# Moving one transposition, one reciprocal and one subtraction in an attention and MLP kernel on Trainium2

## The chip, the cores and the metric

The kernel runs on one core of one Trainium2 chip. The metric is the device time of one execution in microseconds (us), the median of three runs. The engines are TensorE (PE, with its weight loads shown apart as PEld), VectorE (DVE), ScalarE (ACT), GpSimd (POOL) and SyncE (SP), which issues all DMAs of this kernel.

## What is computed

Three stages follow each other: an attention with a relative-position bias, and two MLP mixers. Only the attention bears on this change.

```python
scores = scale * np.matmul(q, k.transpose(0, 1, 3, 2))      # B=4, H=8, S=576, D=64
x = (psi_rel / psi_i)[..., None]
h = np.maximum(x @ w1 + b1, 0.0)                            # hidden = 32
bias = h @ w2                                               # one value per head and pair of positions
scores = scores + bias.transpose(2, 0, 1)[None, :, :, :]
scores = scores - np.max(scores, axis=-1, keepdims=True)
attn = np.exp(scores)
attn = attn / (np.sum(attn, axis=-1, keepdims=True) + 1e-09)
out = np.matmul(attn, v)
```

The MLP weights arrive as 64-bit floats. The kernel rebuilds 32-bit floats from the two words and then splits each weight into a high part (rounded to fp32r) and a low part (the difference), for products in three terms.

## The kernel before

**Units and passes.** The attention is cut into 80 units. A unit is one pair of heads of one batch and one block of 128 rows (the last block of a sequence, index NM, has 64 rows, and both heads then share one tile). The first batch has the units 0 to 19, in the order of `order0`: the 64-row block first, all four pairs of heads, then the next block. The main loop (line 608) runs n from -3 to 80. A pass n does, in this order of the program: the reciprocal and normalisation of unit n+2 (`normalise`, line 459), the scores and minima of unit n+3 (`scores`, line 422), the transpositions of unit n (`turn`, line 482), the transposition of q for unit n+5 (`q_turn`, line 389; first batch only, later batches transpose q on VectorE), the exponentials of unit n+3 (`softmax`, line 450), and the products with v of unit n-1 (`values`, line 507) with their placement in X (`place`, line 415).

**Signs.** The scores are kept negated, so the maximum is a minimum: L443 adds the bias to the scores in PSUM and takes the row minimum, once for each head of a unit. L454 is the exponential with its sum, L460 adds the small constant to the sum on GpSimd, L461 is the reciprocal on VectorE, and L467 scales the rows on GpSimd.

**The bias.** It is built once, in 36 groups of 16 positions. `hidden` (line 315) makes the hidden layer of a group, three of four parts on VectorE (L325) and one on ScalarE (L327); `bias_product` (line 340) multiplies it by w2 on TensorE (L344) into a PSUM tile; `bias_place` (line 352) evicts that tile on ScalarE (L357) and sends it by DMA on SP to `bias_m` or `bias_t`. Six groups are done ahead of the loop, then two in each of the passes -3 to 11 (`gs`).

**PSUM tiles.** `s_tile` (line 333) hands out two tiles `s0` and `s1` of two banks each in turn, to the scores and to the bias products alike; for a unit of two heads `scores` starts again with `s0`, so the scores take `s0` and `s1` and the two bias groups of the pass again `s0` and `s1`. The tile `z` (line 621) holds the transposition of a unit's last columns in `z[:, 0]` and the transposed q in `z[:, 1]`. `values` takes the tags `o` and `z` for its two results (line 514), so it needs z free again. The names `q` and `z` in rows of the trace are these tiles: L394 transposes q into z, L404 copies it out, L487 transposes the unit's last columns into z and L488 copies them out.

**Order on the engines.** Every engine runs its instructions in the order of the program; the kernel sets that order by hand and only waits are added. In a pass with bias groups ScalarE runs: the copy of z (L488), of x (L495), of q (L404), the first exponential (L454), the two evictions (L357), the second exponential, the copy of a values result (L419), two parts of hidden layers (L327). TensorE runs: scores (L435), z, x, y (L487, L494, L500), q (L394), products of both groups (L344), values (L519 to L526).

**Weight parts.** `Jobs` (line 62) prepares MLP weights in pieces between passes. A job of 64-bit weights is four pieces of work on VectorE (L121, L127, L131, L136) and a square on ScalarE (L120). `finish` (line 95) makes the high and low part by `split` (line 57): L59 on ScalarE rounds, L60 subtracts, in `finish` on GpSimd. It is called in the second piece of the next job, ahead of L127:

```python
                yield
                self.finish()
                V.scalar_tensor_tensor(
                    out=wi_, in0=up_, scalar=-0x40000000, in1=wi_, op0=ALU.bitwise_and, op1=ALU.bitwise_or
                )
```

During the attention seven jobs run: three parts of the first weight (`t1`), in the passes from 28 on whose n - 20 is 0 or 3 modulo 5, and four parts of the second (`t2`), one or two pieces a pass from pass 72 on. The first two of them are finished in the passes 40 and 50. The jobs of the later stages (`c1`, `c2`, `wi`, `wo`) use the same class.

Of the kernel before, what the change touches and what calls it, by code (L numbers as in the profile page):

```python
# [7 lines left out]
F32 = mybir.dt.float32  # L8
# [11 lines left out]
def kernel(ctx, tc, ins, consts, out, dbg=None, nb=4, stop=None):  # L20
# [41 lines left out]
    class Jobs:  # L62


        def __init__(self, stg, ahead):
            self.stg, self.ahead = stg, ahead
            self.queue, self.loaded, self.next, self.open, self.gen = [], {}, 0, None, None
            self.done = set()

        def add(self, key, nm, rows, cols, fold, dst, times=1):  # L70

# [23 lines left out]
        def finish(self):  # L95
            if self.open is None:
                return
            key, wf, dst = self.open
            hi, lo = dst()
            if len(hi.shape) == 3:  # L100
                wf = wf.rearrange("p (a b) -> p a b", a=hi.shape[1])
            split(wf, hi, lo, G)
            self.done.add(key)
            self.open = None

# [227 lines left out]
    def s_tile(name):  # L333
        flip[0] ^= 1
        return ps_s.tile([P, 2, 512], F32, tag=f"s{1 - flip[0]}", name=name)
# [1 line left out]
    t = pp.tile([P, 2 * N + TL], F32, tag="p", name="early")  # L337
    early = {groups[2 * j + 1]: t[:, j * N:(j + 1) * N] for j in range(2)}

    def bias_product(gi, hs):  # L340
        ps = s_tile("bps")
        for c in range(4):
            for hf in range(2):
                T.matmul(  # L344
                    ps[32 * c:32 * c + 32, hf, 0:HN],
                    lhsT=w2b.rearrange("p g h -> p (g h)"),
                    rhs=hs[c][:, hf * HN:(hf + 1) * HN],
                    start=True, stop=True, tile_position=(0, 32 * c),
                )
        return ps  # L350
# [35 lines left out]
        V.transpose(out=kt, in_=kraw.pop((b, p)))  # L386
        keys[b, p] = kt

    def q_turn(n, z):

        b, p, it = units[n]
        w = P if it < NM else TL
        if b == 0:
            T.transpose(z[:, 1, 0:w], qraw.pop((b, p, it)), ident[0:w, 0:w])  # L394
        else:
            queries[n] = turned(b, p)[:, it * P:it * P + w]

    def q_out(n, z):
        b, p, it = units[n]
        if b > 0:  # L400
            return
        w = P if it < NM else TL
        t = hl_p.tile([P, P], F32, tag="q0", name="q0", bufs=5)[:, 0:w]
        S.copy(out=rows(t, w), in_=dealt(z[:, 1, 0:w], w))  # L404
        queries[n] = t


# [11 lines left out]
        S.copy(out=out, in_=b)  # L419
        return lambda: V.tensor_tensor(out=out, in0=a, in1=out, op=ALU.add)  # L420

    def scores(n):
        b, p, it = units[n]
        qt, kt = queries.pop(n), keys[b, p]
        na = 2 if it < NM else 1
        if na == 2:
            flip[0] = 0
        ss = [s_tile("ss") for a in range(na)]

        for hf in range(2):  # L430
            js = slice(hf * HN, (hf + 1) * HN)
            for m in range(na):
                for a in range(2):
                    r, o = halves[a], halves[m if na == 2 else a]
                    T.matmul(  # L435
                        ss[a % na][o, hf, 0:HN], lhsT=qt[r, m * HD:(m + 1) * HD], rhs=kt[r, js], start=True, stop=True
                    )
        bias = [bias_m[:, it, 2 * p + a] for a in range(2)] if na == 2 else [bias_t[:, p]]
        pr = pp.tile([P, 2 * N + TL], F32, tag="p", name="pr")
        mn = sm_p.tile([P, 2], F32, tag="mn", name="mn")  # L440
        sm = sm_p.tile([P, 2], F32, tag="sm", name="sm")
        for a in range(na):
            V.tensor_tensor_reduce(  # L443
                out=pr[:, a * NB:a * NB + N].rearrange("p (f n) -> p f n", f=2), in0=ss[a][:, :, 0:HN],
                in1=bias[a].rearrange("p (f n) -> p f n", f=2),
                scale=scale, scalar=BIG, op0=ALU.add, op1=ALU.min, accum_out=mn[:, a:a + 1],
            )
        return pr, mn, sm, na

    def softmax(pr, mn, sm, na, which):  # L450
# [105 lines left out]
    for gi in range(GUP):  # L556
# [10 lines left out]
            k_parts0(p, hl_p if p < 2 else first, "" if p < 2 else "x")  # L567
        if gi >= GUP - 2:
            u = gi - (GUP - 2)
            z = ps_t.tile([P, 2, P], F32, tag="z", name="z")  # L570
            q_turn(u, z)
            q_out(u, z)
    bias_place(groups[GUP - 1], bps)
    gnext = GUP

# [32 lines left out]
    for n in range(-3, U + 1):  # L608
        gs = []
        if n >= -3 and gnext < GALL:  # L610
            gs = list(range(gnext, min(gnext + 2, GALL)))
            gnext += 2
        if 0 <= n + 2 < U:
            normalise(*st[n + 2])
        if 0 <= n + 3 < U:
            st[n + 3] = scores(n + 3)
        if len(gs) > 0:
            hide(gs[0] + 2)
        if n == U - 1:
            values(n - 1)()  # L620
        z = ps_t.tile([P, 2, P], F32, tag="z", name="z") if n < U else None
        if n == U - 1:
            early_x([NM])
        if 0 <= n < U:
# [8 lines left out]
        if n == U - 1:  # L633
            wjobs.need(("t1", NM // 2))
            ph0 = [s_tile("ph")[:, 0] for m in range(NTT)]
            tok1(x0, 0, ph0[0])
        if 0 <= n + 5 < U:
            q_turn(n + 5, z)
        bp = [bias_product(gi, hs.pop(gi)) for gi in gs]
        if 0 <= n + 5 < U:  # L640
            q_out(n + 5, z)
        if 0 <= n + 3 < U:
            softmax(*st[n + 3], which=(0,))
        if 0 <= n < U and n != U - 2:
            y_out(ys, y)
        for gi, x in zip(gs, bp):
            bias_place(groups[gi], x)

        late = 0 < n < U - 1 or n == U
        if late and not gs:  # L650
# [73 lines left out]
    while wjobs.gen is not None or wjobs.next < len(wjobs.queue):  # L724
        wjobs.step()
    wjobs.finish()
    for m in range(1, NTT):
        tok1(x0, m, ph0[m])
    for pl in (sm_p, pt_p, pp, hl_p, raw_p, apool):
# [566 lines left out]
```

## Time and profile before

| what | value |
|---|---|
| median of 3 runs | 903.33 us (903.23 to 903.37) |
| profiled execution | 903.33 us, span 901.5 us |
| PE busy | 885.4 us (98%) |
| PEld busy | 767.9 us (85%) |
| DVE busy | 614.2 us (68%) |
| ACT busy | 421.8 us (47%) |
| POOL busy | 301.3 us (33%) |
| granted TensorE clock | 1.000 |

The span runs from the first to the last instruction; the execution's time has a little around it. Busy shares are of the whole span, over stages that differ: the attention takes the first 320 us or so, the first MLP goes to about 685 us, the second to the end. A busy PE row counts a matmul from its start to its modelled end, and matmuls overlap, so it isn't PE at its peak. In a timeline each row has the start, the duration, engine, line, operation, names and shapes, and in brackets how long the engine was idle before it and what ended that.

### The profile page before, as it was taken

Reading aid. Unit: us, or ns where it says so; the run is one execution under the profiler, and the core shown is the slowest. Engines: PE = TensorE matmul, PEld = TensorE weight load, DVE = VectorE, ACT = ScalarE, POOL = GpSimd, SP = SyncE. Lnnn points to the kernel's source line nnn. Section 1 sums busy time; section 2 is a strip of 40 time slices with the busy share of each in tenths; the row PEclk is TensorE's granted clock in tenths of the full one; section 3 lists DMA queues with packets and bytes.
Section 4 is the critical chain, followed back from the end, with each engine's and each line's share of the span. In section 5 each row is a group of like instructions: output and inputs, shape, how many; then the busy total and the mean of one; then the engine's idle time right before and its main releaser. Section 6 shows DMA issues by size and latency. Waiting matters only on the chain.

```text
span 901.5 us, 22183 instructions
## 1 busy us (share of the span) xinstructions
PE 885.4 (98%) x8962; PEld 767.9 (85%) x8962; DVE 614.2 (68%) x1392; ACT 421.8 (47%) x955; POOL 301.3 (33%) x529
## 2 busy tenths in 40 slices
PE   9999999999999999999999999999999999999998
PEld 4456777767677688999999999999998989889996
DVE  7888677878777779888825353332316999896756
ACT  7999887777777754334312121211115523222310
POOL 1244566666666713133300001001002452423230
PEclk9999999999999999999999999999999999999999
DMA  8956443324323123224300100000041001010002
GB/s 187 198 122 131 92 108 55 72 57 77 64 44 68 32 68 103 85 98 130 127 1 24 47 24 24 33 15 1 1 79 47 24 1 47 1 59 1 1 13 93
DMA packets 120006, 55.39 MB, mean 61 GB/s; under 512 B 101856, under 2 KB 108640, under 8 KB 119904
## 3 DMA queue, kind: packets, MB, share of 16 engines
q1 hardware_dynamic: 119904, 53.98, 24.9%
q8 instruction: 70, 1.15, 0.5%
q14 instruction: 32, 0.26, 0.1%
HBM read 38.62 MB, written 4.72 MB: 48 GB/s over the span
## 4 chain that ended last, share of the span: by engine, by line
PE 75%; DVE 15%; ACT 6%; issue 2%; POOL 1%; DMA 0%; SPq 0%; ACTq 0%; DVEq 0%; POOLq 0%
PE a L931 14%; PE pg L768 14%; PE ss L435 8%; PE o L519 7%; PE po L1148 4%; PE pv L1042 4%; PE ps L1117 4%; PE bps L344 3%; PE x L494 3%; PE pu L1095 3%; PE y L500 3%; DVE res L886 2%; PE z L487 2%; DVE w L131 2%; ACT X L327 1%
## 5 line engine op out<-in xcount | busy, mean ns | idle before, releaser
L931 PE MATMUL a<-g,c 128*128 128x384 f32 x864 | 162.4, 335 | 1.8 <-DVE X L939 1.0
L931 PEld LDWEIGHTS a<-g,c 128*128 128x128 f32 x864 | 150.9, 188 | 3.4 <-ACT g L774 2.2
L775 DVE SCALAR_TENSOR_TENSOR g<-pg,g 128x384 fp32r<-128x384 f32 x72 | 40.0, 556 | 163.7 <-ACT g L774 163.7
L768 PE MATMUL pg<-u,c 128*128 128x384 f32 x720 | 134.4, 334 | 0.0
L467 POOL TENSOR_SCALAR pr<-pr,sm 128x576 f32<-128x576 f32 (+2 forms) x208 | 120.9, 599 | 29.9 <-DVE sm L461 27.9
L768 PEld LDWEIGHTS pg<-u,c 128*128 128x128 f32 x720 | 125.6, 188 | 0.1
L774 ACT ACTIVATE g<-pg 128x384 fp32r<-128x384 f32 x72 | 35.3, 491 | 192.2 <-PE pg L768 192.2
L454 ACT ACTIVATE pr<-pr,mn 128x576 f32<-128x576 f32 x144 | 111.8, 777 | 8.8 <-DVE mn L443 7.6
L443 DVE CUSTOM_DVE_ANT_0 pr<-ss,bias_m 128x576 f32<-128x576 f32 x128 | 90.8, 747 | 2.4 <-ACT X L327 1.8
L519 PE MATMUL o<-xA,vm 64*64 64x128 f32 (+1 forms) x1280 | 82.7, 265 | 0.0
L435 PE MATMUL ss<-kt,X 64*64 64x288 f32 x864 | 77.3, 408 | 2.2 <-DVE mn L443 2.1
L519 PEld LDWEIGHTS o<-xA,vm 64*64 64x64 f32 x1280 | 64.3, 133 | 17.6 <-issue 11.5
L520 PE MATMUL o<-yA,vm 64*64 64x128 f32 x1024 | 71.7, 276 | 0.0
L886 DVE STREAM_TRANSPOSE res<-X 32x256 f32<-32x256 f32 (+1 forms) x176 | 68.2, 387 | 2.7
L60 POOL TENSOR_TENSOR wi<-w,wi 128x512 fp32r<-128x512 f32 x8 | 14.0, 1752 | 153.0 <-DVE g L775 112.5
L60 POOL TENSOR_TENSOR c<-w,c 128x512 fp32r<-128x512 f32 x24 | 35.5, 1480 | 87.3 <-ACT c L59 77.1
L1117 PE MATMUL ps<-wsT,vn 128*128 128x288 f32 x384 | 56.6, 296 | 1.1 <-DVE tmp L1127 1.1
L520 PEld LDWEIGHTS o<-yA,vm 64*64 64x64 f32 x1024 | 55.5, 132 | 0.0
L120 ACT ACTIVATE sq<-wraw 128x512 f32<-128x512 f32 (+2 forms) x43 | 27.8, 646 | 56.7 <-DVE w L136 54.7
L1117 PEld LDWEIGHTS ps<-wsT,vn 128*128 128x128 f32 x384 | 52.7, 188 | 1.9 <-DVE tmp L1127 1.8
L495 ACT COPY xA<-x 128x512 f32<-128x512 f32 x80 | 47.0, 588 | 11.5 <-PE x L494 11.1
L1095 PEld LDWEIGHTS pu<-y,wi 128*128 128x128 f32 x384 | 51.4, 188 | 0.3
(160 smaller groups left out, 1745.0 us busy)
## 6 DMA issues: line engine op xcount, KB each, us to landing
wraw<-in_moe_w_ch_dram SPq DMA_DIRECT2D x24, 512.0 KB, 3.6
bias_m<-bst SPq DMA_DIRECT2D x32, 288.0 KB, 4.0
vm<-in_v_dram SPq DMA_DIRECT2D x32, 128.0 KB, 3.3
wraw<-in_moe_w_in_dram SPq DMA_DIRECT2D x8, 512.0 KB, 3.6
out_dram<-res SPq DMA_DIRECT2D x16, 256.0 KB, 2.0
kr<-in_k_dram SPq DMA_DIRECT2D x48, 72.0 KB, 2.4
qr<-in_q_dram SPq DMA_DIRECT2D x48, 72.0 KB, 2.5
wraw<-in_moe_w_out_dram SPq DMA_DIRECT2D x4, 512.0 KB, 3.3
```

The costliest lines, as they stand in the source:

```text
L60: (eng or V).tensor_tensor(out=lo, in0=src, in1=hi.bitcast(F32), op=ALU.subtract)
L435: T.matmul(ss[a % na][o, hf, 0:HN], lhsT=qt[r, m * HD:(m + 1) * HD], rhs=kt[r, js], start=True, stop=True)
L443: V.tensor_tensor_reduce(out=pr[:, a * NB:a * NB + N].rearrange("p (f n) -> p f n", f=2), in0=ss[a][:, :, 0:HN], in1=bias[a].rearrange("p ...
L454: S.activation(out=pr[:, a * NB:a * NB + N], in_=pr[:, a * NB:a * NB + N], func=AF.Exp, scale=-1.0, bias=mn[:, a:a + 1], accum_out=sm[:, a ...
L467: G.tensor_scalar(out=pr[:, dc:dc + hi - lo], in0=pr[:, lo:hi], scalar1=sm[:, a:a + 1], scalar2=1.0, op0=ALU.mult, op1=ALU.mult,)
L519: T.matmul(o[0:HD, 0:w], lhsT=vm[r, t, 0], rhs=xs[r, t, 0:w], start=st_, stop=en)
L520: T.matmul(o[HD:P, 0:w], lhsT=vm[r, t, 1], rhs=rh[r], start=st_, stop=en)
L768: T.matmul(pg, lhsT=c1[f][i][:, d], rhs=u[j][:, d], start=d == 0 and n == 0, stop=d == ND - 1 and n == 2)
L886: V.transpose(out=o, in_=src(c)[32 * a:32 * a + 32])
L931: T.matmul(acc[d], lhsT=c2[f][i][:, d * P:(d + 1) * P], rhs=g[j], start=f == f0 and n == 0, stop=f == f1 and n == 2,)
L1095: T.matmul(pu[:, hf, 0:HN], lhsT=wi[i][:, d, f * P:(f + 1) * P], rhs=y[j][:, d, js], start=d == 0 and m == 0, stop=d == ND - 1 and m == 2,)
L1117: T.matmul(ps[:, hf, 0:HN], lhsT=vn[i][:, t, ds_], rhs=wsT[j][:, t, js], start=t == 0 and m == 0, stop=False,)
```

## The change

Three edits.

1. The transposed q of the first batch (units n+5 below U0 = 20) no longer lies in `z[:, 1]` but in the tile of the pass's first bias group, in columns 288 to 416 of its first bank, which the products leave free. It is transposed ahead of those products, and its copy to SBUF comes behind the eviction of the first group; in the passes 12 to 14, which have no bias group, the transposition has an `s_tile` of its own and the copy comes right behind. The tile z has one half only.
2. `normalise` of unit n+2 is called between the two minima of unit n+3, not ahead of `scores`.
3. `Jobs` subtracts on VectorE until the attention is over, and on GpSimd from there on.

```diff
@@ class Jobs
             self.done = set()
+            self.eng = V
...
-            split(wf, hi, lo, G)
+            split(wf, hi, lo, self.eng)
@@ bias_product
-    def bias_product(gi, hs):
-        ps = s_tile("bps")
+    def bias_product(gi, hs, ps=None):
+        ps = s_tile("bps") if ps is None else ps
@@ q_turn, q_out
-            T.transpose(z[:, 1, 0:w], qraw.pop((b, p, it)), ident[0:w, 0:w])
+            T.transpose(zq[:, 0:w], qraw.pop((b, p, it)), ident[0:w, 0:w])
...
-        S.copy(out=rows(t, w), in_=dealt(z[:, 1, 0:w], w))
+        S.copy(out=rows(t, w), in_=dealt(zq[:, 0:w], w))
@@ scores
-    def scores(n):
+    def scores(n, between):
...
+            if a == 0:
+                between()
         return pr, mn, sm, na
@@ main loop
-        if 0 <= n + 2 < U:
-            normalise(*st[n + 2])
+        ahead = (lambda: normalise(*st[n + 2])) if 0 <= n + 2 < U else (lambda: None)
         if 0 <= n + 3 < U:
-            st[n + 3] = scores(n + 3)
+            st[n + 3] = scores(n + 3, ahead)
+        else:
+            ahead()
...
-        z = ps_t.tile([P, 2, P], F32, tag="z", name="z") if n < U else None
+        z = ps_t.tile([P, 1, P], F32, tag="z", name="z") if n < U else None
...
+        qs = s_tile("bps") if 0 <= n + 5 < U0 else None
+        zq = None if qs is None else qs[:, 0, HN:HN + P]
         if 0 <= n + 5 < U:
-            q_turn(n + 5, z)
-        bp = [bias_product(gi, hs.pop(gi)) for gi in gs]
-        if 0 <= n + 5 < U:
-            q_out(n + 5, z)
+            q_turn(n + 5, zq)
+        bp = [bias_product(gi, hs.pop(gi), qs if gi == gs[0] else None) for gi in gs]
+        if qs is not None and not gs:
+            q_out(n + 5, zq)
         if 0 <= n + 3 < U:
             softmax(*st[n + 3], which=(0,))
         if 0 <= n < U and n != U - 2:
             y_out(ys, y)
-        for gi, x in zip(gs, bp):
-            bias_place(groups[gi], x)
+        for gi, ps in zip(gs, bp):
+            bias_place(groups[gi], ps)
+            if gi == gs[0]:
+                q_out(n + 5, zq)
@@ behind the attention
     wjobs.finish()
+    wjobs.eng = G
```

The two transpositions of q ahead of the loop use a tile of one half with the same tag; nothing else changes there.

## Rows read from the trace of the kernel before

**Rows 1.** Busy time by stretches: engine, busy us, instructions, then clock, DMA share, GB/s.

```profile
50.00:75.00 25.00, 24.80 (x441) 16.22 (x440) 21.88 (x55) 23.77 (x54) 10.42 (x24) 1.00 0.48 112
```

**Rows 2.** Chain of waits in order of time, 59 to 71.5 us: start, us, what.

```profile
65.34 2.17 PE bps L344 x32
...
67.53 0.83 ACT bst L357
...
70.51 0.26 ACT zA L488
...
70.82 0.33 PE z L394
```

**Rows 3.** Timeline of TensorE: the first transposition of some passes.

```profile
40.69 0.30 PE L487 MATMUL z<-ident,pr 128*64 128x128 f32 x1
...
92.80 0.33 PE L487 MATMUL z<-ident,pr 128*128 128x128 f32 x1
98.36 0.33 PE L487 MATMUL z<-ident,pr 128*128 128x128 f32 x1
...
109.68 0.33 PE L487 MATMUL z<-ident,pr 128*128 128x128 f32 x1
...
189.54 0.33 PE L487 MATMUL z<-ident,pr 128*128 128x128 f32 x1
192.79 0.33 PE L487 MATMUL z<-ident,pr 128*128 128x128 f32 x1
197.97 0.30 PE L487 MATMUL z<-ident,pr 128*64 128x128 f32 x1
```

**Rows 4.** Timeline of TensorE's weight loads, passes 6, 11 and 12.

```profile
65.00 0.14 PEld L394 LDWEIGHTS z<-ident,qm 128*128 128x128 f32 x1 [0.31 <-ACT zA L488]
...
93.73 0.14 PEld L394 LDWEIGHTS z<-ident,qm 128*128 128x128 f32 x1
...
100.03 0.13 PEld L519 LDWEIGHTS o<-xA,vm 64*64 64x64 f32 x1 [0.23 <-ACT q L404]
```

**Rows 5.** Timeline of VectorE, minima in the passes 6 and 13.

```profile
64.52 0.08 DVE L443 DVE_READ_ACCUMULATOR2_ANT mn<- 128x1 f32 x1
...
103.07 0.76 DVE L443 CUSTOM_DVE_ANT_0 pr<-ss,bias_m 128x576 f32<-128x576 f32 x1 [0.17 <-PE x L494]
```

**Rows 6.** Timeline of ScalarE, passes 12 and 73.

```profile
99.71 0.27 ACT L404 COPY q<-z 128x128 f32<-128x128 f32 x1
...
300.96 0.40 ACT L59 CAST t<-w 128x256 fp32r<-128x256 f32 x1
```

**Rows 7.** Chain of waits in order of time, 190 to 202 us.

```profile
193.06 0.53 ACT t L59
...
193.72 1.27 POOL t L60
...
195.37 0.74 DVE pr L443
```

**Rows 8.** Timeline of VectorE, passes 40, 41 and 74.

```profile
192.54 0.68 DVE L127 SCALAR_TENSOR_TENSOR w<-wraw,w 128x512 int32<-128x512 int32 x1
195.28 0.17 DVE L461 RECIPROCAL sm<-sm 128x2 f32<-128x2 f32 x1 [2.07 <-POOL sm L460]
...
302.54 0.17 DVE L461 RECIPROCAL sm<-sm 128x2 f32<-128x2 f32 x1 [1.30 <-POOL sm L460]
```

**Rows 9.** Line 60 over the whole span: count, ns min/median/max, first and last start.

```profile
L60 DVE TENSOR_TENSOR x<-px,x x15: 674/683/684, 330.4 to 368.3; 128x512 fp32r<-128x512 f32 x12, 64x512 fp32r<-64x512 f32 x3
...
L60 DVE TENSOR_TENSOR wsT<-wst,wsT x10: 415/416/457, 690.1 to 704.7; 128x288 fp32r<-128x288 f32 x10
```

**Rows 10.** Timeline of VectorE, passes 75 and 79, the bit operation of 288 columns.

```profile
308.43 0.45 DVE L131 SCALAR_TENSOR_TENSOR w<-wraw,w 128x288 int32<-128x288 int32 x1
...
322.91 0.99 DVE L131 SCALAR_TENSOR_TENSOR w<-wraw,w 128x288 int32<-128x288 int32 x1
```

**Rows 11.** Timeline of GpSimd, pass 79.

```profile
322.78 0.81 POOL L60 TENSOR_TENSOR t<-w,t 128x288 fp32r<-128x288 f32 x1 [5.85 <-ACT t L59]
```

More of the change, by code (lines that the diff above doesn't have):

```diff
@@ L387, in k_turn, with q_turn @@
         keys[b, p] = kt
-    def q_turn(n, z):
+    def q_turn(n, zq):
         b, p, it = units[n]
@@ L393, in q_turn, with q_out @@
         if b == 0:
-            T.transpose(z[:, 1, 0:w], qraw.pop((b, p, it)), ident[0:w, 0:w])
+            T.transpose(zq[:, 0:w], qraw.pop((b, p, it)), ident[0:w, 0:w])
         else:
             queries[n] = turned(b, p)[:, it * P:it * P + w]
-    def q_out(n, z):
+    def q_out(n, zq):
         b, p, it = units[n]
@@ L569 @@
             u = gi - (GUP - 2)
-            z = ps_t.tile([P, 2, P], F32, tag="z", name="z")
-            q_turn(u, z)
-            q_out(u, z)
+            zq = ps_t.tile([P, P], F32, tag="z", name="zq")
+            q_turn(u, zq)
+            q_out(u, zq)
     bias_place(groups[GUP - 1], bps)
```

## The prediction

> **What bounds the kernel now.** I read the granted clock first (1.0 throughout, so no stage is slowed by it), then the busy table by stretches, then the chain of waits in two stretches of the attention, then the starts of L487 on TensorE, which open each pass of the loop over units and so give the length of a pass, and last the timelines of ScalarE, VectorE and GpSimd inside single passes. I call a pass by its n; the first start of L487 is n = 0, and it has one row per pass.
>
> Passes -3 to 11 also carry two bias groups each. There TensorE looks full, but ScalarE is nearly as full: 23.77 of 25 us [rows 1]. The chain in this stretch is a ring [rows 2]: the products of the two groups (65.34, 2.17 us), ScalarE's eviction of the second (67.53), ScalarE's further work up to the copy of z (70.51), q's transposition L394 (70.82), and the next products. Q's transposition closes the ring only because it writes the second half of the tile z whose first half ScalarE copies: it is held 0.31 us by that copy [rows 4]. Nine passes, n = 2 to 10, take 92.80 - 40.69 = 52.11 us, 5.79 each [rows 3]. The pass after them has the same products, and its q did not wait [rows 4]; it took 98.36 - 92.80 = 5.56.
>
> Passes 12 to 14 transpose q without bias groups: 109.68 - 98.36 = 11.32, 3.77 each. Later passes have neither and run at TensorE's own pace, 192.79 - 189.54 = 3.25 [rows 3]. In passes 12 to 14 the values (L519, 100.03) start only behind the copy of q out of z (99.71, 0.27), because they reuse z [rows 4, 6].
>
> Two later passes are broken by a weight part: n = 41 takes 197.97 - 192.79 = 5.18, and n = 51 repeats it. There [rows 7] ScalarE's cast ends at 193.59, GpSimd's subtraction takes 1.27, the small add in front of the reciprocal queues behind it on GpSimd, the reciprocal waits 2.07 us on VectorE [rows 8], the first minimum behind it starts at 195.37, and the scores wait for the minimum to free their PSUM tile. So 5.18 - 3.25 = 1.93 us are lost in each.
>
> The profiled execution took 903.33 us, which is the median of the three runs; its span is 901.5, so 1.8 us lie around it. Everything below is taken off 903.33. The work after the attention keeps its instructions and is set going by the attention's end, so I carry a gain there through to the end one for one.
>
> **Part 1, q in the bias tile.** It removes nothing: 20 transpositions and 20 copies stay, of which 18 move. It removes two waits and adds one: the transposition now needs the bias tile free, which means the first minimum must have read its scores. In passes 2 to 10 that read is over at 64.52 + 0.08 = 64.60 [rows 5], and without its wait the transposition would start at 65.00 - 0.31 = 64.69: it just fits. Queued behind that wait on TensorE are the products, which need the same tile anyway. The copy of q moves on ScalarE from before the first exponential to between the two evictions. The second eviction waits there for the second group's products (it starts at 67.53, the products end at 65.34 + 2.17 = 67.51), so the copy hides in that gap; without the gap it would cost its 0.27 again. No DMA is issued by it, and the DMAs of the bias groups keep their place on SP.
>
> Bounds for a pass: nothing, if another engine closes the ring at the same length; 0.31, the wait itself. ScalarE's load gives 23.77 / 25 x 5.79 = 5.51 as a floor, and the pass that had no wait gives 5.56. I take 5.55, since that pass is the nearest row: 9 x (5.79 - 5.55) = 2.2 us, with ends 0 and 2.8. Passes -3 to 1 have units of 64 rows and wait more for evictions than for z: 0.1, ends 0 and 0.5.
>
> In passes 12 to 14 the values no longer wait for q's copy. Over the 3.25 of a plain pass there are 0.52 us, of which q's own transposition keeps at most 0.33 [rows 2]. So 0.19 at least if nothing else is late, and 0.4 if the transposition overlaps its neighbours. But in pass 13 the first minimum starts at 103.07 and runs 0.76 [rows 5], 0.17 after its reciprocal was done, on something that the trace doesn't name; if that stays, q waits for it to 103.87, later than the values start now, and the gain of two passes is gone. I take 0.3 x 3 = 0.9, ends 0 and 1.2.
>
> **Part 2, the reciprocal between the minima.** Same 80 instructions. The first minimum no longer stands behind a reciprocal that waits for GpSimd. In plain passes TensorE sets the pace, so this gives nothing; it matters where the small add is late, and it frees the bias tile sooner in part 1. What it adds: the second minimum now queues behind the reciprocal (0.17) and its wait, and the second exponential behind that. GpSimd's normalisation starts up to one minimum later, 0.74 us [rows 7]; its product is used by transpositions two passes, over 6 us, later, and that distance hides it. Without that cover it would cost up to 0.74 a pass. Taken as 0.
>
> **Part 3, the subtraction on VectorE.** Seven subtractions fall in the attention: two of 512 columns and one of 256 for the first weight, four of 288 for the second. VectorE's own rows for this line are 0.68 us at 512 (from PSUM) and 0.42 at 288 [rows 9]. The wait that it adds is for ScalarE's cast; VectorE stands still in order, and behind it wait the weight's next bit operation, the next minimum, and then the scores.
>
> For n = 40 to 41: the cast ends at 193.59, the subtraction then ends at 194.3, the bit operation that ran at 192.54 (0.68) [rows 8] comes behind it and ends at about 194.9, and the first minimum starts there and not at 195.37. That is 0.45 earlier, not 1.93, because VectorE takes over a part of the wait. Two of them: 0.9, ends 0 (as late as today) and 3.9 (all that is lost).
>
> For the 256 columns: the cast ends at 300.96 + 0.40 = 301.36 [rows 6], and before this change the reciprocal ran at 302.54 and the minimum behind it [rows 8]. After: 301.36 + 0.42 + two bit operations of 0.45 [rows 10] and an add between them, about 302.8. So the first minimum comes as late as today or 0.2 later. The first of 288 has the same shape; the last three lie under the transpositions and the long products at the end of the attention. Together a loss of 0.2, ends a loss of 1.5 and a gain of 1.0.
>
> Sum: 2.2 + 0.1 + 0.9 + 0.9 - 0.2 = 3.9, so **899.4 us**.
>
> **What speaks against part 3.** VectorE's bit operation of 288 columns takes 0.45 us alone and 0.99 when it starts under GpSimd's 0.81 us subtraction [rows 10, 11]: two engines on one store hold each other up for the whole instruction. The Trainium skill ("SBUF — State Buffer", Who interferes with whom) says that a VectorE instruction with two SBUF inputs and a GpSimd instruction that reads SBUF shut each other out, the later one until the earlier is done; the two rows agree. The subtraction is such an instruction and it now meets GpSimd's normalisations.
>
> **Rivals.** *The ring closes elsewhere* (no change): ScalarE's 5.5 us, or the bias tile that comes free 0.09 before it is wanted, hold the passes near 5.75. Then part 1 gives 9 x 0.05 + 0.3, part 3 0.5, in all 1.2: 902.1. For it: four engines stand within 0.3 us of each other. Against: the pass at 92.80. Chance 0.14.
>
> *The weights' stalls go whole* (larger gain): with GpSimd free, the reciprocal and both minima come early, and 1.5 more of each 1.93 is regained: 899.4 - 3.0 = 896.4. Against: VectorE's own order, worked out above. Chance 0.11.
>
> *The subtraction holds VectorE* (slower): each of the seven meets a normalisation and loses about 0.54 us (0.99 - 0.45), with the wait for the cast that now stands on VectorE ahead of the minima. The two large ones then gain nothing (2 x (0.45 - 0.54) = -0.2), the next two lose 0.2 + 0.54 each (-1.5), the last three 0.54 and the cast's 0.4 (-2.8): -4.5 together, and with part 1 at 2.0 the time is 905.8. It decides when each subtraction costs the path over 0.6 us net. Against: GpSimd waits for the reciprocal just when the subtraction runs. Chance 0.05.
>
> **How the numbers follow.** My forecast has 0.70 and spans 897.5 to 901.4. The range reaches 0.6 into the larger gain and up to the no-change case: 896.8 to 902.2. A measurement here can tell 0.2%, 1.8 us, from no change, so faster means under 901.5: 0.70 + 0.11 = 0.81; same 0.14; slower 0.05.
>
> **What would show it.** Right: passes 2 to 10 near 5.55, no wait of q's transposition on the copy of z, passes 12 to 14 near 3.5, n = 41 and 51 near 4.7, later passes still 3.25, the chain around 194 through VectorE's subtraction. Wrong: q's transposition waiting for the first minimum, scores waiting longer for the second eviction, or VectorE subtractions above 1 us ahead of a late minimum.

## The result and the profile after

The changed kernel takes 894.46 us (median of 4 runs, 894.25 to 895.05) where the kernel before takes 903.35 on the same chip: a ratio of 0.9902 [0.9885, 0.9919], 8.9 us less. The forecast was 899.4 with a range down to 896.8, so the sign and the order of size were right and the gain was more than twice the 3.9 us forecast.

| | before | after |
|---|---|---|
| profiled execution, span (us) | 903.33, 901.5 | 894.58, 892.8 |
| PE busy (us) | 885.4 | 878.1 |
| DVE busy (us) | 614.2 | 621.9 |
| ACT busy (us) | 421.8 | 417.6 |
| POOL busy (us) | 301.3 | 297.7 |
| last pass begins (last z transposition, us) | 320.89 | 311.92 |
| from there to the end of the span (us) | 580.6 | 580.9 |

The last two lines come first in the reading: the whole gain is made before the last pass of the attention (8.97 us) and is carried to the end almost one for one (0.3 lost). The question is only which passes became shorter. Line numbers have moved: after the change z is L490, the minima L444, the small add L463, the reciprocal L464, the scores L436, q's transposition L395 and its copy L405, the bias product L345.

The first transposition of some passes on TensorE, kernel after (start, duration, what), in the view of [rows 3]:

```profile
41.02 0.30 PE L490 MATMUL z<-ident,pr 128*64 128x128 f32 x1
...
90.60 0.33 PE L490 MATMUL z<-ident,pr 128*128 128x128 f32 x1
...
96.16 0.33 PE L490 MATMUL z<-ident,pr 128*128 128x128 f32 x1
...
106.63 0.33 PE L490 MATMUL z<-ident,pr 128*128 128x128 f32 x1
...
126.15 0.33 PE L490 MATMUL z<-ident,pr 128*128 128x128 f32 x1
...
129.40 0.30 PE L490 MATMUL z<-ident,pr 128*64 128x128 f32 x1
...
132.22 0.33 PE L490 MATMUL z<-ident,pr 128*128 128x128 f32 x1
...
187.74 0.33 PE L490 MATMUL z<-ident,pr 128*128 128x128 f32 x1
192.44 0.30 PE L490 MATMUL z<-ident,pr 128*64 128x128 f32 x1
```

Passes 2 to 10 now take (90.60 - 41.02) / 9 = 5.51 and not 5.79; passes 12 to 14 take 10.47 / 3 = 3.49 and not 3.77; n = 41 takes 4.70 and not 5.18. These were forecast. The pair n = 21, 22 was not. It takes 3.25 + 2.82 here; in the kernel before it takes 3.34 + 3.18, from its own rows in the same view:

```profile
129.31 0.33 PE L487 MATMUL z<-ident,pr 128*128 128x128 f32 x1
...
132.65 0.30 PE L487 MATMUL z<-ident,pr 128*64 128x128 f32 x1
...
135.83 0.33 PE L487 MATMUL z<-ident,pr 128*128 128x128 f32 x1
```

The row with 128*64 is a unit of 64 rows, one in every five. Its pass has no y transpositions, and in the one behind it the products of the values are narrower, so both can be short (2.82 here, in n = 22 and 23). I call n = 22, 27, ..., 72, the units' own, the short passes. The same account for the whole attention:

| passes | change (us) |
|---|---|
| start of the span to the first bias-free pass (n = 12): +0.65 up to the first z, -2.85 from there | -2.20 |
| 12 to 14 | -0.85 |
| 15 to 20 | -0.11 |
| 41, 42, 51, 52 (a weight part falls in 41 and 51) | -1.56 |
| the other plain passes (no bias groups, no weight part finished) from 21 to 73 | **-4.47** |
| 74, 76 (the 256 columns and the first of 288) | +0.22 |
| sum, at the last z | -8.97 |

The bold line is half of the result, and the prediction had a zero there. 4.10 of it lies in nine pairs like 21 and 22, the rest in n = 35, 45 and 73, which took 3.33, 3.42 and 2.96 before and 3.25, 3.25 and 2.83 now.

Where the 0.45 us of a pair went is seen in the timeline of VectorE and of the weight loads. First VectorE of the kernel before, in pass 22:

```profile
133.14 0.17 DVE L461 RECIPROCAL sm<-sm 128x2 f32<-128x2 f32 x1 [0.82 <-POOL sm L460]
133.23 0.74 DVE L443 CUSTOM_DVE_ANT_0 pr<-ss,bias_m 128x576 f32<-128x576 f32 x1
133.89 0.08 DVE L443 DVE_READ_ACCUMULATOR2_ANT mn<- 128x1 f32 x1
133.89 0.75 DVE L443 CUSTOM_DVE_ANT_0 pr<-ss,bias_m 128x576 f32<-128x576 f32 x1
134.57 0.08 DVE L443 DVE_READ_ACCUMULATOR2_ANT mn<- 128x1 f32 x1
```

and its weight loads for the scores, in the same pass:

```profile
134.30 0.19 PEld L435 LDWEIGHTS ss<-kt,X 64*64 64x64 f32 x2
134.70 0.69 PEld L435 LDWEIGHTS ss<-kt,X 64*64 64x64 f32 x14 [0.21 <-DVE mn L443]
```

VectorE stands 0.82 us idle for GpSimd's small add, with both minima queued behind a reciprocal of 0.17. The second minimum ends at 134.6, and only then has the scores' PSUM tile been read out; TensorE, which in a short pass has less to do, is already there with the next scores and waits. The sixteen loads end at 135.39, 2.74 us after the pass's z. VectorE of the kernel after, same pass:

```profile
129.52 0.76 DVE L444 CUSTOM_DVE_ANT_0 pr<-ss,bias_m 128x576 f32<-128x576 f32 x1 [0.37 <-PE ss L436]
130.21 0.08 DVE L444 DVE_READ_ACCUMULATOR2_ANT mn<- 128x1 f32 x1
130.21 0.16 DVE L464 RECIPROCAL sm<-sm 128x2 f32<-128x2 f32 x1
130.28 0.74 DVE L444 CUSTOM_DVE_ANT_0 pr<-ss,bias_m 128x576 f32<-128x576 f32 x1
```

and its weight loads:

```profile
131.05 0.72 PEld L436 LDWEIGHTS ss<-kt,X 64*64 64x64 f32 x16
```

Now the first minimum waits for TensorE's scores, 0.37 us, and the reciprocal behind it finds its sum ready. From the short pass's z, the first minimum starts 0.12 us later (129.52 - 129.40) where it started 0.58 later (133.23 - 132.65), and the 16 loads of the scores run in one piece without a wait and end 2.37 us after the z (131.77 - 129.40). That is the 0.36 us of n = 22; the other 0.09 of the pair lie in n = 21.

In the bias passes the chain of waits of the kernel after, 55 to 68 us, names only TensorE; around q's transposition it reads (start, us, what):

```profile
63.75 0.44 PE y L503 x4
64.19 0.11 PE bps L395
64.30 2.11 PE bps L345 x32
```

The ring of [rows 2] through ScalarE's eviction and its copy of z is gone. By stretches (the columns of [rows 1]) TensorE's busy time fills the 25 us:

```profile
50.00:75.00 25.00, 25.00 (x449) 16.88 (x442) 24.32 (x61) 24.34 (x56) 11.72 (x25) 1.00 0.54 127
```

### The profile page after: what moved, and what is told of

It is laid out like the page before. It is cut to its first block, busy times and chain, and to the rows that moved or that the text cites. A ratio compares the mean times of both kernels' runs of the same rounds, so it can differ in the third digit from the quotient of the medians.

```text
span 892.8 us, 22187 instructions
## 1 busy us (share of the span) xinstructions
PE 878.1 (98%) x8962; PEld 762.3 (85%) x8962; DVE 621.9 (70%) x1399; ACT 417.6 (47%) x955; POOL 297.7 (33%) x522
## 4 chain that ended last, share of the span: by engine, by line
PE 76%; DVE 16%; ACT 3%; issue 3%; DMA 1%; SPq 0%; DVEq 0%; ACTq 0%
PE a L941 14%; PE pg L778 14%; PE ss L436 8%; PE o L522 7%; PE po L1158 4%; PE pv L1052 4%; PE ps L1127 4%; PE x L497 3%; PE bps L345 3%; PE pu L1105 3%; PE y L503 3%; DVE res L896 2%; PE z L490 2%; DVE w L132 2%; DVE w L128 2%
## 5 line engine op out<-in xcount | busy, mean ns | idle before, releaser
L470 POOL TENSOR_SCALAR pr<-pr,sm 128x576 f32<-128x576 f32 (+2 forms) x208 | 126.5, 626 | 60.8 <-DVE sm L464 55.4
L444 DVE CUSTOM_DVE_ANT_0 pr<-ss,bias_m 128x576 f32<-128x576 f32 x128 | 95.5, 746 | 14.1 <-PE ss L436 11.7
L436 PE MATMUL ss<-kt,X 64*64 64x288 f32 x864 | 72.5, 405 | 0.8 <-DVE mn L444 0.7
L326 DVE TENSOR_SCALAR X<-ttab,wsm 128x576 f32<-128x576 f32 x108 | 55.2, 572 | 0.1
```

Of the source, the lines that this page charges most:

```text
L326: V.tensor_scalar(out=hd, in0=tt, scalar1=b1i, scalar2=None, op0=ALU.min)
L436: T.matmul(ss[a % na][o, hf, 0:HN], lhsT=qt[r, m * HD:(m + 1) * HD], rhs=kt[r, js], start=True, stop=True)
L444: V.tensor_tensor_reduce(out=pr[:, a * NB:a * NB + N].rearrange("p (f n) -> p f n", f=2), in0=ss[a][:, :, 0:HN], in1=bias[a].rearrange("p ...
L470: G.tensor_scalar(out=pr[:, dc:dc + hi - lo], in0=pr[:, lo:hi], scalar1=sm[:, a:a + 1], scalar2=1.0, op0=ALU.mult, op1=ALU.mult,)
```

## The experiments

Two theories stood after the result. **O, the order**: the 4.5 us in the plain passes come from the first minimum no longer standing behind the reciprocal, and show in the short passes, where TensorE is early. **L, the load**: they come from what parts 1 and 3 take off (GpSimd without the subtraction, a smaller z), and the order is beside the point. The first five runs take the three parts alone and in pairs; the rest vary one place each. All ratios are to the kernel before (903.3 to 903.4).

### The parts alone

**Part 2 alone**, on the kernel before:

```diff
-        if 0 <= n + 2 < U:
-            normalise(*st[n + 2])
+        ahead = (lambda: normalise(*st[n + 2])) if 0 <= n + 2 < U else (lambda: None)
         if 0 <= n + 3 < U:
-            st[n + 3] = scores(n + 3)
+            st[n + 3] = scores(n + 3, ahead)
+        else:
+            ahead()
```

> The kernel before with part 2 alone: the reciprocal and normalisation between the two minima; q stays in z, GpSimd subtracts. Theory O (order): what the prediction missed, some 5 us, is that in the short passes (64-row unit, from pass 22 on, 11 of them) the scores wait for minima that stand behind the reciprocal. Then this alone takes 11 x 0.45 = 5.0 us, and about 1.2 more in the two passes with a weight's subtraction, where the first minimum no longer waits for GpSimd: 897.2 us, passes 21 and 22 together 6.07 and not 6.52. Rival L (load): the gain in the plain passes comes from GpSimd relieved of the subtraction or from z being shorter; then this gives under 1 us, 902.5 or more, and passes 21 and 22 stay at 6.5.

Measured: 896.33 us, 0.9923 [0.9908, 0.9938]. Passes 21 and 22 take 3.25 + 2.81, as in the kernel after; passes 2 to 14 are as before. The starts of n = 21, 22 and 23 on TensorE:

```profile
129.55 0.33 PE L489 MATMUL z<-ident,pr 128*128 128x128 f32 x1
132.80 0.30 PE L489 MATMUL z<-ident,pr 128*64 128x128 f32 x1
135.61 0.33 PE L489 MATMUL z<-ident,pr 128*128 128x128 f32 x1
```

Passes 41 and 51 take 4.51 and 4.50, and n = 76 takes 2.81 where it took 3.76. So the part that I had costed at nothing gives 7.0 of the 8.9 us alone.

**Part 1 alone** is the kernel after with both of these edits, which undo parts 2 and 3:

```diff
-            self.eng = V
+            self.eng = G
...
         if 0 <= n + 3 < U:
+            ahead()
+            ahead = lambda: None
             st[n + 3] = scores(n + 3, ahead)
```

> The changed kernel with parts 2 and 3 undone: only q in the bias tile. Both theories expect 1.5 to 2.2 us from passes 2 to 10. In passes 12 to 14 the bias tile comes free later, since the first minimum stands behind the reciprocal again: theory O expects 0.4 there in all, not 0.85, so 901.0 us and passes 21 and 22 at 6.5 together. Rival L in its form with z expects 6.1 for these two and 896.

Measured: 902.0 us (10 runs, 901.29 to 904.41), 0.9985 [0.9976, 0.9995]. The plain passes are those of the kernel before (6.52 for 21 and 22). Passes 2 to 10 reach 5.46 to 5.52, but n = 5 and n = 9 take 5.64 and 5.74, and n = 13 and 14 take 4.20 and 3.92, longer than the 3.77 of before, so that the passes 12 to 14 lose 0.16 together where 0.4 of gain was expected. With the old order the minima are late in some passes, and here q waits for the bias tile behind them, 0.23 us in n = 9 and in n = 13 and 14:

```profile
101.43 0.14 PEld L395 LDWEIGHTS bps<-ident,qm 128*128 128x128 f32 x1 [0.86 <-DVE mn L444]
105.35 0.14 PEld L395 LDWEIGHTS bps<-ident,qm 128*128 128x128 f32 x1 [0.58 <-DVE mn L444]
```

That is the wait the prediction said part 1 adds. Against the kernel after, it loses 0.11, 0.20, 0.46 and 0.56 in n = 5, 9, 13 and 14.

**Part 3 alone**, on the kernel before:

```diff
-            split(wf, hi, lo, G)
+            split(wf, hi, lo, self.eng)
```

> The kernel before with part 3 alone: VectorE subtracts in the attention. Theory O: about 0.5 in each of the passes 41 and 51, a loss of 0.2 at pass 74, plain passes unchanged: 902.5 us. Rival L: with GpSimd free the plain passes shorten, passes 21 and 22 together near 6.1, and about 898 us.

Measured: 902.45 us, 0.999 [0.9981, 0.9999]. n = 41 and 51 take 4.70 and 4.43 (5.18 before), n = 74 and 76 take 4.33 and 3.87 (4.27 and 3.76). The pair 21, 22 stays at 6.52. With this and the run before it, L has fallen: neither of the two parts touches the plain passes.

### Two parts of three

**Parts 1 and 3**, the kernel after with the reciprocal ahead of both minima again:

```diff
         if 0 <= n + 3 < U:
+            ahead()
+            ahead = lambda: None
             st[n + 3] = scores(n + 3, ahead)
```

> The changed kernel with part 2 alone undone: parts 1 and 3 together. Theory O: the sum of q alone and subtraction alone, 900.2 us, with passes 21 and 22 at 6.5; against the changed kernel it is 5.7 us slower. Rival L: near the changed kernel, 895.

Measured: 900.84 us, 0.9972 [0.9963, 0.9982]; 21 and 22 take 6.51, n = 13 and 14 take 4.20 and 3.92. 6.4 us of the change are lost by one order of three instructions.

**Parts 1 and 2**, the kernel after with the subtraction back on GpSimd:

```diff
-            self.eng = V
+            self.eng = G
```

> The changed kernel with part 3 undone: q in the bias tile, the reciprocal between the minima, GpSimd subtracts. Theory O2: once the first minimum no longer stands behind the reciprocal, the subtraction on VectorE costs more than it saves, because it holds the first minimum where GpSimd's holds only the second; e1 had 4.51, 4.50, 4.08 and 2.81 in the passes 41, 51, 74 and 76 where the changed kernel has 4.70, 4.44, 4.45 and 3.80. So this is 1.2 us faster than the changed kernel: 893.2 us. Rival: the three parts add up, each by its own gain (7.0 + 1.5 + 0.85 is near the whole 8.9), and without part 3 it is 0.85 slower: 895.3.

Measured: 893.01 us (892.77 to 894.2), 0.9887 [0.9873, 0.9902]: 1.45 us **less** than the kernel after. So part 3 gains 0.9 on the kernel before and loses 1.45 on top of parts 1 and 2; on spans, 892.8 against 891.4. The intervals of the two ratios overlap, so the loss rests on the lengths of single passes in the traces. VectorE of this kernel in pass 41:

```profile
188.08 0.75 DVE L444 CUSTOM_DVE_ANT_0 pr<-ss,bias_m 128x576 f32<-128x576 f32 x1
...
190.23 0.17 DVE L464 RECIPROCAL sm<-sm 128x2 f32<-128x2 f32 x1 [1.39 <-POOL sm L463]
190.31 0.74 DVE L444 CUSTOM_DVE_ANT_0 pr<-ss,bias_m 128x576 f32<-128x576 f32 x1
```

and VectorE of the kernel after in the same pass:

```profile
188.56 0.69 DVE L60 TENSOR_TENSOR t<-w,t 128x512 fp32r<-128x512 f32 x1 [0.98 <-ACT t L59]
189.16 0.68 DVE L128 SCALAR_TENSOR_TENSOR w<-wraw,w 128x512 int32<-128x512 int32 x1
189.77 0.75 DVE L444 CUSTOM_DVE_ANT_0 pr<-ss,bias_m 128x576 f32<-128x576 f32 x1
```

With GpSimd subtracting, only the reciprocal and the second minimum are late (190.31), and the first half of the next scores can go (the first two loads are there at 189.85, the others wait 1.07 us). With VectorE subtracting, VectorE waits 0.98 us for ScalarE's cast, and both minima stand behind that wait, the subtraction and a bit operation. In n = 41 the two come out 0.20 apart, in n = 51 0.07 the other way. The difference is made at the 256 and 288 columns: n = 74 takes 4.10 with GpSimd and 4.45 with VectorE, n = 76 2.82 and 3.80, n = 77 3.05 and 2.81. In n = 76 VectorE of the kernel after waits for the cast again:

```profile
300.09 0.46 DVE L60 TENSOR_TENSOR t<-w,t 128x288 fp32r<-128x288 f32 x1 [1.19 <-ACT t L59]
...
301.40 0.75 DVE L444 CUSTOM_DVE_ANT_0 pr<-ss,bias_t 128x576 f32<-128x576 f32 x1
```

With GpSimd subtracting the same minimum stands at

```profile
299.52 0.74 DVE L444 CUSTOM_DVE_ANT_0 pr<-ss,bias_t 128x576 f32<-128x576 f32 x1
```

Counted from the pass's z (299.47 and 298.98) it starts 1.93 us behind it in the one kernel and 0.54 in the other. This unit has 64 rows and one minimum only, so the reciprocal holds none.

### The order, place by place

**The old order in the short passes alone**:

```diff
         if 0 <= n + 3 < U:
+            if n >= U0 and 0 <= n < U and units[n][2] == NM:
+                ahead()
+                ahead = lambda: None
             st[n + 3] = scores(n + 3, ahead)
```

> The changed kernel with the reciprocal ahead of the first minimum again in 12 passes only: those from pass 20 on that transpose a 64-row unit (22, 27, ..., 72 and the last). Theory O: nearly the whole of what the prediction missed sits there, since only there TensorE comes to the scores before the minima are done; 11 x 0.36 = 4.0 us come back: 898.5 us, and pass 21 stays at 3.25 while 22 goes back to 3.18. If the place of the reciprocal matters in all passes alike, only 12 of 80 shares of 7 us come back: 895.5 us.

The edit reaches 11 passes and not 12: the last 64-row unit is transposed in n = 79, which makes no scores any more.

Measured: 899.95 us, 0.9963 [0.995, 0.9976]. This is 5.5 us above the kernel after, where 4.0 was expected. Each of the nine pairs like 21, 22 takes about 0.47 longer (58.79 for all nine, against 54.59), n = 42 and 52 take 3.54 and 3.53 where they took 2.87 and 2.86, and the other passes keep their length. VectorE of this kernel in pass 22 and its weight loads:

```profile
129.82 0.17 DVE L464 RECIPROCAL sm<-sm 128x2 f32<-128x2 f32 x1 [0.83 <-POOL sm L463]
```

```profile
130.89 0.19 PEld L436 LDWEIGHTS ss<-kt,X 64*64 64x64 f32 x2
131.38 0.69 PEld L436 LDWEIGHTS ss<-kt,X 64*64 64x64 f32 x14 [0.30 <-DVE mn L444]
```

The reciprocal's wait of 0.83 and the scores' wait for the minimum are both back, in a kernel that has everything else of the change. Pass 21 keeps 3.25 as expected, and n = 22 takes 3.27, so the pair is back at 6.52. The short passes decide; O stands. The nine pairs give 4.2 us, and n = 42 and 52 lose 0.67 each besides, which makes the 5.5. They follow a weight part, and there VectorE waits longer for the same add, 1.23 us:

```profile
195.03 0.17 DVE L464 RECIPROCAL sm<-sm 128x2 f32<-128x2 f32 x1 [1.23 <-POOL sm L463]
```

**The reciprocal behind both minima** tells whether its place between them matters, or only that it isn't ahead of the first:

```diff
-            if a == 0:
-                between()
+        between()
```

> The changed kernel with the reciprocal behind both minima. If all that counts is that no minimum stands behind a reciprocal that waits for GpSimd, plain passes stay at 3.25, 2.82 and 2.83, and only passes where GpSimd or the sum is late can gain: 894.2 us, within 0.5 of the changed kernel. If GpSimd's normalisation, which starts 0.7 us later still, comes too late for its transposition, passes lengthen and it is 896 or more.

Measured: 894.02 us, 0.9899 [0.9883, 0.9916]. The plain passes are the same; n = 41 and 51 take 4.64 and 4.37, n = 42 and 52 2.81 and 2.82. What counts is that the first minimum doesn't wait for GpSimd; between or behind differ by less than these runs can tell.

### What part 3 costs: the wait for the cast

**The cast one piece earlier.** A weight part is worked off in pieces. The split (ScalarE's cast, then the subtraction) belongs to one piece; here the cast is issued behind the square of the piece before, and VectorE still subtracts:

```diff
                 S.activation(out=sq[r, 0:n], in_=up_.bitcast(F32), func=AF.Square)
+                self.high()
```

where `high` is the split's `S.copy(out=hi, in_=wf)`.

> The changed kernel, but ScalarE casts a weight's high part one piece earlier, so that VectorE's subtraction finds it done and doesn't stand still. If the price of part 3 is VectorE waiting for the cast, the passes 41 and 51 come down to 3.6 or less, 74 and 76 to about 3.0, and the time to 891 us. If it is the subtraction's own length on VectorE (0.69), they come down by little, and the time stays at 893.5 or more.

Measured: 891.23 us (891.0 to 892.12), 0.9868 [0.9852, 0.9884], 3.2 us below the kernel after. n = 41 and 51 take 3.63 and 3.36, n = 74 3.63 (3.0 was expected), n = 76 2.81; n = 39 and 49, where the cast now runs, take 3.66 and 3.42, against 3.25. VectorE in pass 41:

```profile
187.54 0.68 DVE L113 TENSOR_TENSOR t<-w,t 128x512 fp32r<-128x512 f32 x1
188.14 0.69 DVE L145 SCALAR_TENSOR_TENSOR w<-wraw,w 128x512 int32<-128x512 int32 x1
188.74 0.75 DVE L461 CUSTOM_DVE_ANT_0 pr<-ss,bias_m 128x576 f32<-128x576 f32 x1
```

The 0.98 wait is gone and the first minimum starts 0.95 us behind the pass's z (187.79) and not 2.03 (189.77 - 187.74). So most of what part 3 cost was the wait for the cast, 1.07 of the 1.45 by which n = 41 stood over a plain pass. The other 0.38 stay, with the subtraction and the bit operation still ahead of the minimum, and a smaller price is paid two passes earlier: in n = 39 the cast (0.60 us at 181.61) stands on ScalarE ahead of the copy of z, which starts 1.24 us behind the pass's z and not 0.71.

**The same with GpSimd subtracting**, on top of the early cast:

```diff
-            self.eng = V
+            self.eng, self.early = G, True
...
-            if self.open is None or self.cast is not None or self.eng is not V:
+            if self.open is None or self.cast is not None or not self.early:
```

> As the run with the earlier cast, but GpSimd subtracts, as before the change. If the wait for the cast is the whole price on either engine, this ends within 0.7 us of it, near 891; if GpSimd's 1.27 us in front of the small add matter by themselves, the passes 41 and 51 stay above 4, and the time is 892.5 or more.

Measured: 892.14 us, 0.9877 [0.9862, 0.9891], between the two expectations. n = 41 and 51 take 3.71 and 3.43, n = 74 still 4.09 (3.63 with VectorE), n = 77 3.18 (2.81 with VectorE). With the cast out of the way VectorE is the better place for the subtraction by 0.9 us, which is what part 3 was for; the intervals of the two ratios overlap, and n = 74 and 77 (0.46 and 0.37) carry the difference.

**q back in z in the passes below 0**, on top of the early cast, asked whether q's new place costs anything at the start (the first z came at 30.39 after the change, at 29.74 before):

```diff
-        qs = s_tile("bps") if 0 <= n + 5 < U0 else None
-        zq = None if qs is None else qs[:, 0, HN:HN + P]
+        qs = s_tile("bps") if 0 <= n and n + 5 < U0 else None
+        zq = z[:, 0] if n < 0 else None if qs is None else qs[:, 0, HN:HN + P]
```

> The run with the earlier cast on VectorE, and in the passes -3 to -1, which do not use z for a unit, q stays in z. Part 1 delays the start: the first z comes at 30.39 and not at 29.74, because the scores of the early passes take the tile that q's copy has yet to leave. If that is so, the first z comes back to 29.8 or less and the time falls by 0.3 to 0.6 against the run with the earlier cast alone: 890.8 us. If the delay has another cause, no change: 891.2.

Measured: 890.91 us (890.58 to 891.03), 0.9862 [0.9847, 0.9877]; the first z at 30.06, against 30.11 with the early cast alone. Nothing moved that these runs can tell; the 30.39 that the expectation starts from is that of another kernel. The start differs without q too: 30.08 in the run of part 2 alone. It also differs between two kernels that are the same up to n = 13, 30.39 in the kernel after and 30.10 in the run with another bias at unit 16 below. What sets it stays open. This and the early cast are the fastest kernels of the study.

### Pass 13

n = 13 is the one pass in 12 to 14 that stayed long, 3.74. Its first minimum waits 0.71 us in the kernel after, and the profile names z (L490), which the minimum does not read:

```profile
100.07 0.76 DVE L444 CUSTOM_DVE_ANT_0 pr<-ss,bias_m 128x576 f32<-128x576 f32 x1 [0.71 <-PE z L490]
```

A named releaser that the instruction does not use leaves open what it waited for. A DMA is a candidate: unit 16 is the first to read the last bias group, which is copied to its place on SP at 94.04. This run lets unit 16 read block 2's bias instead:

```diff
-        bias = [bias_m[:, it, 2 * p + a] for a in range(2)] if na == 2 else [bias_t[:, p]]
+        bias = [bias_m[:, 2 if n == 16 else it, 2 * p + a] for a in range(2)] if na == 2 else [bias_t[:, p]]
```

> The changed kernel, where the minima of unit 16 alone add the bias of another block of rows (the third, not the fourth), so that they don't need the last bias group; that part of the result is left different. Pass 13 keeps 3.74 in all kernels with q in the bias tile, 0.38 over its neighbours, since the first minimum waits 0.71 for something that the trace does not name. If it is the landing of the last group's bias, pass 13 falls to 3.37 and the wait is gone; the same wait then shows up at unit 17 at most as a remnant. If it is anything else, 3.74 stays.

Measured: 893.75 us in one run, n = 13 at 3.36. Its minimum:

```profile
99.42 0.76 DVE L444 CUSTOM_DVE_ANT_0 pr<-ss,bias_m 128x576 f32<-128x576 f32 x1 [0.29 <-PE ss L436]
```

It starts 0.12 us behind the pass's z (99.30), where it started 0.54 behind it (100.07 - 99.53), and waits for its scores, as its neighbours do. So the unnamed wait was for the last bias group. SP's queue has the two copies that this concerns, and the view of the DMAs (count, KB each, median us from issue to landing) their group, both in the kernel after:

```profile
94.04 1.51 SPq L364 DMA_DIRECT2D bias_m<-bst  x2
```

```profile
bias_m<-bst SPq DMA_DIRECT2D x32, 288.0 KB, 4.1
```

The second of the two is issued within the 1.51 us from 94.04, so by the median of 4.1 it lands between 98 and 100; the minimum starts at 100.07. I read no row for the landing of this one copy.

## Why the prediction was right or wrong

**Part 1: right in its mechanism, with some luck in its number.** Forecast -2.2 and -0.1 in the bias passes, measured -2.20 up to n = 12. But the passes themselves gave more, 9 x 0.28 = 2.5 in n = 2 to 10 and 0.3 in n = 0 and 1, and a first z that came 0.65 later, for which no cause is shown, took the excess away. 5.55 for a pass was forecast and 5.51 measured. The wait of 0.31 for the copy of z [rows 4] is gone: the loads for q's transposition in pass 12 stand in the kernel after as

```profile
97.09 0.14 PEld L395 LDWEIGHTS bps<-ident,qm 128*128 128x128 f32 x1
...
100.89 0.14 PEld L395 LDWEIGHTS bps<-ident,qm 128*128 128x128 f32 x1 [0.40 <-DVE mn L444]
```

The second row is pass 13. In passes 12 to 14, -0.9 was forecast (3 x 0.3) and -0.85 came, which is luck in part, since two misses cancel: -0.4 in two of them and -0.03 in the pass whose first minimum is late. That risk was named, with the right place (q waits for that minimum); the cause, the bias group's landing, was not in the trace read then. Part 1 alone does not give this sum, however: 1.3 us in all. It needs the order of part 2, which makes the bias tile free early (the waits of 0.86 and 0.58 above are 0.40 and none with it); the prediction saw the tie ("it frees the bias tile sooner in part 1") and put no number on it. Across the measured medians, part 1 is worth 1.3 alone and 896.33 - 893.01 = 3.3 on top of part 2.

**Part 2: the step that failed.** It reads "In plain passes TensorE sets the pace, so this gives nothing", and "Taken as 0". Measured: -4.47 in the plain passes and -0.11 in 15 to 20; and part 2 alone also shortens n = 41 and 51 by 0.67 each. Put -4.5 for the zero and the forecast is 894.9, 0.4 from the measured 894.46; this is nearer than the terms deserve, since the stalls at the weight parts, booked under part 3, were also taken away by part 2. The mistake is in a reading: I took 3.25 from one pass, n = 40 [rows 3], and let it stand for all plain passes. The list of starts, read in fives, shows 3.25, 3.25, 3.34, 3.18, 2.83 in the kernel before. The 2.83 is TensorE's own pace behind a 64-row unit, and the 3.18 right ahead of it is the short pass, held up; the weight loads of the scores there (the 0.21 behind the minimum) name the holder. The 0.82 wait of the reciprocal was also seen only where it was 2.07, at the weight parts [rows 8], and read as the effect of GpSimd's subtraction; it stands in the plain passes too, without any subtraction: in n = 22 GpSimd itself waits 0.41 us for ScalarE's exponential and begins its add of 0.19 us at 132.92, just ahead of the reciprocal at 133.14.

**What part 2 was said to add** did not bite: the second minimum behind the reciprocal and the later normalisation leave no pass longer in the kernel after (with part 2 alone n = 77 takes 3.04 and not 2.81). The cover named, the two passes between a normalisation and its transpositions, held.

**Part 3: right where it stood alone.** In n = 41 and 51 the forecast was near 4.7, and 4.70 and 4.44 came (4.70 and 4.43 in part 3 alone; n = 51 is the shorter because the bit operation behind its subtraction has 256 columns and takes 0.42 us, not 0.68). In n = 74 and 76, +0.2 was forecast and +0.22 measured. Alone it gave 0.85 us where the prediction has 0.9 - 0.2. But it was costed against the old order. With part 2 in place, n = 41 takes 4.50 without part 3 and n = 76 takes 2.82, so the same part costs 1.45. The prediction added its three parts as if each met the kernel before; part 2 had already taken away what part 3 was to gain, and left its wait.

**The rivals.** *The ring closes elsewhere* fell: every pass from 2 to 10 takes 5.46 to 5.54. The reading given for it was wrong as well: by [rows 1] only TensorE (24.80) and ScalarE (23.77) stand within 0.3 us of each other in a pass, VectorE's 21.88 of 25 make 5.07 of 5.79. *The weights' stalls go whole* named a time nearer to the measured one (896.4) by another mechanism; the stalls went by 0.48 and 0.74 of 1.93. With the cast moved ahead these two passes do come down almost whole (3.63 and 3.36), though n = 39 and 49 pay 0.41 and 0.17 for it; what was mostly in the way was the wait for the cast. *The subtraction holds VectorE* was right in kind, since part 3 does lose by holding the minima, and wrong in its means: no subtraction was stretched. The seven are in the kernel after, by count, minimum, median and maximum in ns:

```profile
L60 DVE TENSOR_TENSOR t<-w,t x7: 425/459/693, 188.6 to 317.2; 128x288 fp32r<-128x288 f32 x4, 128x512 fp32r<-128x512 f32 x2, 128x256 fp32r<-128x256 f32 x1
```

against 0.42 and 0.68 us in [rows 9]. GpSimd stands waiting for the reciprocal while the two of 512 columns run, as argued. The next three meet small instructions of GpSimd, and it is these that take longer: its add 0.37 us at 292.44 and 0.41 at 300.20 against a median of 0.19, its copies (L494) from 306.34 up to 0.50 against 0.23. So the 0.45 us of the bit operation at 308.43 [rows 10] was not "alone" either: GpSimd's two copies beside it, from 307.93, took 1.04 and not 0.52. What does meet the normalisations is the last instruction of a weight part (L137, two inputs in SBUF), in the kernel before as well (0.92 us at 311.65). In the kernel after it is stretched at 295.56, under a normalisation that runs from 294.47 to 296.17, and not at 309.58, beside no GpSimd instruction:

```profile
295.56 0.92 DVE L137 SCALAR_TENSOR_TENSOR w<-sq,w 128x288 f32<-128x288 f32 x1
...
309.58 0.45 DVE L137 SCALAR_TENSOR_TENSOR w<-sq,w 128x288 f32<-128x288 f32 x1
```

The rule of the Trainium skill ("SBUF — State Buffer", Who interferes with whom), by which two such instructions shut each other out, agrees with the pair.

## What to carry to other kernels

Read the length of every pass, not of one: a period in the list of starts (here every fifth unit is half as tall) separates an engine's own pace from a wait that hides under the longer passes, and a "98% busy" engine can still be waiting in one pass of five. On an engine that works in order, put an instruction that waits for another engine behind the one whose data is ready and whose result frees a buffer; 0.17 us of reciprocal ahead of two minima was worth 7 us of 903. When parts of a change touch the same queue, cost them in the order in which they would be added, since the second may gain what the first has already taken, and keep only its own wait.

## What the runs showed that I had not expected

A change of engine that was right against one order of instructions was wrong against another: -0.85 us on the kernel before, +1.45 on top of parts 1 and 2, and again -0.9 (892.14 to 891.23) once the cast came earlier. The last two differences are within overlapping intervals and rest on the same passes of the traces. The start of the attention moves by up to 0.7 us between kernels that do the same work there (first z at 29.74 to 30.41), without a cause that any run shows; gains of that size should be read from later intervals and not from absolute times.
